# Eleven-product up-projections in two thirds of nine groups, with one room for gates and rotated rows from the fifth unit on

## The chip, the cores and the metric

The kernel runs on one core of a Trainium2 chip. The metric is the device time of one execution in microseconds (us). A core has TensorE (PE: matrix products into PSUM), VectorE (DVE) and ScalarE (ACT) for elementwise work, GpSimd (POOL), SyncE (SP), which here only issues transfers, and 16 DMA engines.

## The reference

A gated linear recurrence feeds a gated feed-forward block, all in 32-bit floats. There are 4 sequences of 768 steps, 8 heads of 48 features; the feed-forward has 3072 tokens, 384 model features and 1536 inner ones.

```
scale = min(mag, 0.999) / (mag + 1e-6)          # mag = |a_re + i a_im|
S = (a * scale) * S + k v^T                     # complex state, per step and head
y = q . Re(S)
x  = y as (3072, 384);  xn = x / rms(x) * rms_g
out = (silu(xn @ w_gate) * (xn @ w_val)) @ w_out
```

## The kernel before

The steps of the recurrence are cut into 24 chunks of 128 tokens (C = 128). Two chunks make a *unit* for the recurrence (the first two units are single chunks, so there are 13) and a *group* for the feed-forward (12 groups of T = 256 tokens).

**A unit.** `load_gates` brings a_re and a_im into the tiles re and im (L674, three transfers each, from SP). `load_rows` brings k, q (L741) and, per chunk, v (L748). `gates` turns re and im by a long chain of ACT and DVE steps on 128x768 elements into cumulated magnitudes and angles: it begins with Square of re (L783), later writes qs at L798, and ends with four products, rot0 to rot3, that rotate k and q into ks, qs, k and q (DVE, L610, the last one `q<-q,y`). `move_rows` copies the rotated rows by 12 transfers a unit into kr and qr (L879), which have features on partitions. Working tiles such as s, w, y, ks and qs have one room each, so the chain of the next unit waits at L798 until the rows of this one have moved. re and im have two rooms, and so have kr and qr: a move waits only for the last y of the unit before the previous one (L888).

**A chunk.** `scores` makes s_ps (PE, L1072), masks it (am, DVE L1077) and transposes kr (kt_ps, L1093). `finish` makes the state (state_ps, L1115, carried on by DVE) and y_ps (L1144). `normalise` makes the root mean square (rs on POOL, L1180) and xT, the scaled input of the feed-forward (DVE, L613); two xT rooms exist, so xT of group g waits for the up-projection of group g-2.

**A group.** The up-projection has 12 inner tiles f of 128 features. A plain tile (L1345) is three contraction blocks for w_gate (wg) and three for w_val (wv), 256 columns each, in one PSUM room "g" of three; then silu (ACT, L1349) and a product (DVE) give hT. In groups 9 to 11 (ELEVEN = 9) `eleven` treats two tiles at once, a *pair* p: for each of the two weights the first two of the three contraction blocks form a 2x2 by 2x2 block product, made with 7 products of 128 columns where 8 would do it plainly, out of sums of weight blocks (S1 to S4, `eleven_sums`) and differences of xT blocks (T, `eleven_inputs`); the third contraction block stays plain with 256 columns. So a weight's pair takes 7 narrow products and two of double width: eleven blocks of 128 columns where the plain way has twelve. The products come in four phases: `one`, `two`, `three`, `four` (L1260). Between phases a partial sum has to leave PSUM: ACT copies it into R (L1284), and DVE adds to R later. Two pairs run in turn, phase by phase, so that one's copy lies under the other's products. Their PSUM rooms are A (from the three "g") and B (from the five "a", which the recurrence uses too).

The output projection (`project`, L1423, from group 2 on) is the same idea with 7 products P1, P2, P6, P7, P5, P3, P4 of six tiles each, sums S1 to S4 of hT on DVE, and copies (ACT, L1445) and adds into ot. P1 starts when the first six tiles of hT are there. Groups 0 and 1 project plainly (L1372).

**What sets the order.** Every step belongs to a lane; `Order.run` plans the kernel ahead of time on estimated durations. Again and again it takes, of all lanes' next steps, the one that could begin first, with a small lateness of its lane (or of the step, `late`) added, and emits it. So each engine's order is fixed when the kernel is built, and at run time engines only wait for one another. `takes` and `gives` count PSUM rooms. `small` reads the weights again at the end (tile `again`, L1040) and takes minima of them on DVE (L1044) for a final check.

Of the kernel before, what the change touches and what calls it, by code (L numbers as in the profile page):

```python
# [568 lines left out]
def fast(tc, ctx, qT, kT, v, a_re, a_im, w_gate, w_val, w_out, rms_g, out, H, bad):  # L569
# [96 lines left out]

    def gate(name, ap, queue, u):
        first_, m = units[u]
        b, c = divmod(first_, NCH)
        if name not in UN[u]:  # L670
            UN[u].update((x, ours(u, x, bufs=2)) for x in ("re", "im"))
        rows = ap[b].rearrange("(h j l) s -> j l h s", j=ND, l=L)
        for j in range(ND):
            queue.dma_start(out=UN[u][name][:, j], in_=rows[j][:, :, c * C:(c + m) * C])  # L674
# [42 lines left out]

    G = [dict() for _ in range(NG)]
# [3 lines left out]
    def load_gates():  # L722
        for u, (first_, m) in enumerate(units):
            for name, ap in (("re", a_re), ("im", a_im)):
                aside = u < 2 and name == "im"
                if (u, name) == (0, "im"):
                    order.ends[name, u] = 8.0
                    continue
                yield step("ACT" if aside else "SP", 0.0 if aside else 3 * order.ISSUE,
                           [("s", units[slots[u - 3][-1]][0])] if u > 2 else [("q", 1)] if u == 2 else [],  # L730
                           lambda name=name, ap=ap, u=u, q=nc.scalar if aside else nc.sync: gate(name, ap, q, u),
                           mb=0.2 * m, ends=[(name, u)])

    def load_rows():
        for u, (first_, m) in enumerate(units):
# [10 lines left out]
            def value(n):  # L746
                U[n]["v"] = vz[n % 4]
                nc.sync.dma_start(out=vz[n % 4][:, :, 0:D],  # L748
# [5 lines left out]
            for n in range(0 if u == 1 else first_, first_ + m) if u else ():  # L754
                yield step("SP", 0.6, [("y", n - 4) if n > 3 else None], lambda n=n: value(n),
# [8 lines left out]
    ELEVEN = 9  # L764
    UPS, OUTS = 0.05, 0.06
# [103 lines left out]
    def move_rows():  # L869
        for u, (first_, m) in enumerate(units):  # L870
            t, two = UN[u], {}

            def move(i, t=t, u=u, two=two, first_=first_, m=m):
                name, rows = ("kr", "qr")[i % 2], (1 - i // 2) * D
                queue = nc.gpsimd if u < ASIDE and i % 2 else nc.sync
                if i < 2:
                    two[name] = sized(unit, name, H, m, p=D2)
# [7 lines left out]
            for i in range(4):  # L885
                aside = u < ASIDE and i % 2
                yield step("POOL" if aside else "SP", 3 * order.ISSUE,
                           [("rot%d" % i, u), ("y", units[u - 1][0] - 1) if u > 1 else None],  # L888
# [131 lines left out]
    def small():  # L1020

        for i, (to, ap, c, f) in enumerate(parts):
# [5 lines left out]
            for half in range(2):  # L1028
# [9 lines left out]
                def get(k=k, n=n, rows=rows, from_=from_):  # L1038
                    raws[k] = prep.tile([P, n], I32, tag="re", name="again", bufs=2)
                    nc.sync.dma_start(out=raws[k].rearrange("p (c f) -> p c f", c=rows), in_=from_)  # L1040
# [6 lines left out]
                yield step("SP", 0.5, [("moved", NU - 1), ("least", k - 2) if k > 1 else ("piece", len(parts) - 1)],  # L1047
# [163 lines left out]
    def eleven_sums():  # L1211

        for i, to in enumerate((wg, wv)):
            a11, a12, a21, a22 = (to[:, :, d, f * P:(f + 1) * P] for f in range(2) for d in range(2))
            for name, tag, x, y, op in (("S1", ("ks", "qs"), a21, a22, ALU.add), ("S2", ("s", "w"), "S1", a11, ALU.subtract),
                                        ("S3", ("y", "r"), a11, a21, ALU.subtract), ("S4", ("p", "k"), a12, "S2", ALU.subtract)):

                def emit(i=i, name=name, tag=tag[i], x=x, y=y, op=op):
                    o = E[name, i] = prep.tile([P, NW * P], FP32, tag=tag, name=name).rearrange("p (f t) -> p f t", f=NW)
                    tt(o, *(E[z, i] if isinstance(z, str) else z for z in (x, y)), op)  # L1220

                yield step("DVE", tt_us(NW * P), [("moved", NU - 1)], emit, ends=[(name, i)])

    def eleven_inputs():

        for g in range(ELEVEN, NG):
# [3 lines left out]
            def inputs(g=g, t=t):  # L1230
                if "T" not in E:
                    E["T"] = prep.tile([P, ND * T], FP32, tag="q", name="T").rearrange("p (a i c) -> p a i c", a=2, i=ND)
                    E["R"] = [prep.tile([P, ND * T], FP32, tag="im", name="R", bufs=2)
                              .rearrange("p (j w c) -> p j w c", j=ND, w=2) for _ in range(2)]
                b11, b12, b21, b22 = t["b"] = [t["xT"][:, d, i * C:(i + 1) * C] for d in range(2) for i in range(2)]
                t1, t2, t4 = t["T"] = [E["T"][:, g % 2, i] for i in range(3)]
                for o, x, y in ((t1, b12, b11), (t2, b22, t1), (b12, b22, b12), (t4, b21, t2)):
                    tt(o, x, y, ALU.subtract)

            yield step("DVE", 4 * tt_us(C), [("xT", last), ("S4", 1), ("up", g - 2)], inputs,  # L1240
                       ends=[("in", g)])

    def eleven(g):
# [5 lines left out]
        def pair(p):  # L1249
# [4 lines left out]
            def product(to, a, b, start=False, stop=False, at=at, p=p):  # L1254

                bank, j = to
                for i, w_ in enumerate((wg, wv)):
                    left = E[a, i][:, p] if isinstance(a, str) else w_[:, p, a[0], a[1] * P:(a[1] + 1) * P]
# [4 lines left out]
            def one(at=at, product=product):  # L1263
                at["A"] = ps_g.tile([P, 2, 2, C], FP32, tag="g", name="up_ps")
                at["r"] = E["R"][p % 2]
# [3 lines left out]
            def two(at=at, product=product):  # L1269
                product(("A", 1), "S2", t["T"][1])  # L1270
                at["B"] = ps_a.tile([P, 2, 2, C], FP32, tag="a", name="up2_ps")
                product(("B", 1), "S3", t["b"][1], start=True)
# [10 lines left out]
            def copied(j, at=at):  # L1283
                nc.scalar.copy(out=at["r"][:, j], in_=at["A"][:, :, 1])  # L1284

            def add(j, bank, block, at=at):
                tt(at["r"][:, j], at[bank][:, :, block], at["r"][:, j], ALU.add)

            def silu(at=at, f1=f1, f2=f2):
                act_ = nc.scalar.activation  # L1290
                act_(out=h[:, f1, C:], in_=at["A"][:, 0, 1], func=AF.Silu)
                act_(out=h[:, f1, 0:C], in_=at["r"][:, 0, 0], func=AF.Silu)

            def silu2(at=at, f2=f2):
                nc.scalar.activation(out=h[:, f2].rearrange("p (i c) -> p i c", i=2), in_=at["r"][:, 1:3, 0], func=AF.Silu)

            def times(at=at, f1=f1):
                tt(h[:, f1, C:], at["A"][:, 1, 1], h[:, f1, C:])
                tt(h[:, f1, 0:C], at["r"][:, 0, 1], h[:, f1, 0:C])

            def times2(at=at, f2=f2):
                o = h[:, f2].rearrange("p (i c) -> p i c", i=2)
                tt(o, at["r"][:, 1:3, 1], o)
# [3 lines left out]
            o, f = (g, f2) if p > 1 else (g - 1, NF + f2)  # L1307
            free = [("h", o, f - 4), ("h", o, f - 5)] if o >= ELEVEN else []
            yield [step("PE", 2 * us, [("in", g)] + ([("out", g - 2)] if p == 0 else []), one, then=0.2, dense=True,
                        ends=[K("1")], takes=("g", 1))]  # L1310
            yield [step("ACT", ac_us(T), [K("1")] + free, lambda c=copied: c(0), ends=[K("p1")])]
            yield [step("PE", 2 * us, [K("p1")], two, then=0.2, dense=True, ends=[K("2")], takes=("a", 1))]
            yield [step("ACT", ac_us(T), [K("2")], lambda c=copied: c(1), ends=[K("u2")])]
            yield [step("PE", 2 * us, [K("u2")], three, then=0.2, dense=True, ends=[K("3")])]
            yield [step("DVE", tt_us(T), [K("u2")], lambda a=add: a(1, "B", 1), ends=[K("u3")])]
            yield [step("ACT", ac_us(T), [K("3")], lambda c=copied: c(2), ends=[K("u4")])]
            yield [step("PE", us + 4 * 2 * pe_us(T), [K("u4"), K("u3")], four, then=0.2, dense=True,
                        ends=[K("4")] + [("up", g)] * (p == NW - 1))]
            yield [step("DVE", tt_us(T), [K("4")], lambda a=add: a(0, "A", 0), ends=[K("c11")]),
                   step("ACT", 2 * ac_us(C), [K("4"), K("c11")], silu, table=["silu"], ends=[K("s1")]),  # L1320
                   step("DVE", 2 * tt_us(T), [K("4")], lambda a=add: (a(1, "B", 0), a(2, "B", 1)), ends=[K("c2")], gives="a"),
                   step("ACT", ac_us(T), [K("c2")], silu2, table=["silu"], ends=[K("s2")]),
                   step("DVE", 2 * tt_us(C), [K("s1")], times, ends=[("h", g, f1)], gives="g"),
                   step("DVE", tt_us(T), [K("s2")], times2, ends=[("h", g, f2)])]

        for p in range(0, NW, 2):

            two = [list(pair(p + i)) for i in range(2)]
            for phase in zip(*two):
                for steps in phase:  # L1330
                    yield from steps

    def feed_forward(groups):
        for g in groups:
            t = G[g]
            for f in range(NF):

                def tile_(f=f, t=t, g=g):
                    t["hT"] = hT[g % 2]
                    t["gv", f] = ps = ps_g.tile([P, 2, T], FP32, tag="g", name="gv_ps")  # L1340
                    busy(flat(ps))
                    cols = slice(f * P % FW, f * P % FW + P)
                    for i, w_ in enumerate((wg, wv)):
                        for d in range(ND):
                            nc.tensor.matmul(ps[:, i], lhsT=w_[:, f * P // FW, d, cols], rhs=t["xT"][:, d],  # L1345
                                             start=d == 0, stop=d == ND - 1)

                def silu(f=f, t=t):
                    nc.scalar.activation(out=t["hT"][:, f], in_=t["gv", f][:, 0], func=AF.Silu)  # L1349

                def times(f=f, t=t):
                    tt(t["hT"][:, f], t["gv", f][:, 1], t["hT"][:, f])

                w_ = [("piece", 2 * (f * P // FW) + i) for i in range(2)]
                free = ([("piece", x) for x in range(2 * NW) if ROOM[x] in ((6, 7), (0, 1))[g]] if g < 2 else [("out", g - 2)]) if f == 0 else []
                yield step("PE", 12 * pe_us(T), w_ + free + [("xT", g * UC + UC - 1)], tile_, then=0.2, dense=True, fills=True,
                           ends=[("gv", g, f)] + [("up", g)] * (f == NF - 1), takes=("g", 1))
                yield step("ACT", ac_us(T), [("gv", g, f)], silu, table=["silu"], ends=[("silu", g, f)])
                yield step("DVE", 0.15 + T / 960, [("silu", g, f)], times, ends=[("h", g, f)], gives="g")
# [207 lines left out]
```

## Time and profile before

| | |
|---|---|
| median of 14 runs | 767.82 us (762.83 to 773.22) |
| the profiled execution, its own time | 765.71 us |
| its span, first to last instruction | 763.6 us, granted TensorE clock 0.984 |
| VectorE busy | 510.0 us (67%) |
| ScalarE busy | 366.2 us (48%) |
| up-projection, plain tiles on TensorE, x1296 | 160.9 + 157.9 us |
| eleven-product pairs, narrow products of T with S, x144 | 22.0 us, mean 275 ns |
| output projection, 128x192 | 85.9 + 42.5 + 21.2 us |
| mean TensorE busy in 200 to 740 us | 538.75 of 540 us |

A line of the groups view reads: source line, engine, operation, output and inputs by their names in the program, shape and count; then busy time and mean duration in ns; then idle time of the engine just before, and which instruction ended most of it. A line of the waits view reads: who waited for whom, in all, how often, the longest. A line of the timeline reads: start, length, engine, line, operation, and how many instructions were merged; an idle time before it stands in brackets. TensorE instructions overlap, so their pace is the distance between starts. Each 32-bit product shows as two instructions.

### The profile page before, as it was taken

The page shows a single profiled execution, that of the slowest core. Times are in us where ns is not written, and L with a number is a line of the kernel's source. Part 1 is how long each engine was busy: PE and PEld are TensorE (multiplying, and loading weights), DVE is VectorE, ACT ScalarE, POOL GpSimd, SP SyncE. Part 2 cuts the span into 40 slices and gives each one's busy share as a digit, 9 for nine tenths or more (in the row PEclk, how much of TensorE's full clock was granted, in tenths as well). Part 3 has the DMA queues.
Part 4 walks back from the last instruction along what each step waited for, and adds up shares of the span by engine and source line. Part 5 has one row for each costly group of instructions (what it writes and reads, how often), then busy time and mean ns, then how long its engine had stood idle before and what let it go on. Part 6 is the DMA issues. An engine that isn't in the chain of part 4 may idle for free. (4 is left out here: it accounts for less than half of the span.)

```text
span 763.6 us, 13411 instructions
## 1 busy us (share of the span) xinstructions
PE 705.3 (92%) x5294; PEld 631.9 (83%) x5294; DVE 510.0 (67%) x997; ACT 366.2 (48%) x640; POOL 50.6 (7%) x93
## 2 busy tenths in 40 slices
PE   0468889999999999999999999999999999999995
PEld 0256568787778999998899899898989999999985
DVE  3979979595576793854869478584586844756462
ACT  5654475566455635464656644547442113233230
POOL 3323000101000000000000000000000000000000
PEclk9987989999999999999999999999999999999998
DMA  7797970945609217365072831907307233233321
GB/s 221 168 186 189 182 194 2 184 128 81 138 1 126 72 23 105 83 74 134 11 126 74 109 80 26 180 14 91 67 16 90 77 100 107 81 114 103 95 94 67
DMA packets 103335, 76.57 MB, mean 100 GB/s; under 512 B 39328, under 2 KB 98464, under 8 KB 103264
## 3 DMA queue, kind: packets, MB, share of 16 engines
q1 hardware_dynamic: 98656, 60.30, 41.2%
q0 software_dynamic: 3744, 14.94, 7.0%
q8 instruction: 43, 0.70, 0.5%
q10 hardware_dynamic: 864, 0.39, 0.2%
q14 instruction: 28, 0.23, 0.1%
HBM read 51.98 MB, written 4.76 MB: 74 GB/s over the span
## 5 line engine op out<-in xcount | busy, mean ns | idle before, releaser
L1345 PE MATMUL gv_ps<-xT,wg 128*128 128x256 f32 x648 | 160.9, 385 | 1.6 <-DVE hT L610 1.6
L1345 PE MATMUL gv_ps<-xT,wv 128*128 128x256 f32 x648 | 157.9, 380 | 2.6 <-DVE wv L610 2.6
L1345 PEld LDWEIGHTS gv_ps<-xT,wv 128*128 128x128 f32 x648 | 123.4, 191 | 19.9 <-DVE wv L610 3.0
L1345 PEld LDWEIGHTS gv_ps<-xT,wg 128*128 128x128 f32 x648 | 120.3, 191 | 20.0 <-issue 2.9
L1349 ACT ACTIVATE hT<-gv_ps 128x256 f32<-128x256 f32 x108 | 40.8, 384 | 149.6 <-PE gv_ps L1345 149.2
L610 DVE TENSOR_TENSOR hT<-gv_ps,hT 128x256 f32<-128x256 f32 x108 | 44.8, 419 | 82.2 <-ACT hT L1349 81.9
L1423 PE MATMUL out_ps<-wo,hT 128*128 128x192 f32 x480 | 85.9, 329 | 3.0 <-ACT ot L1445 3.0
L1423 PEld LDWEIGHTS out_ps<-wo,hT 128*128 128x128 f32 x480 | 78.0, 190 | 5.1 <-ACT ot L1445 4.4
L1072 PE MATMUL s_ps<-qr,kr 96*128 96x128 f32 x384 | 48.3, 279 | 8.4 <-DMA qr<-q 5.2
L1072 PEld LDWEIGHTS s_ps<-qr,kr 96*128 96x128 f32 x384 | 45.6, 192 | 11.3 <-issue 4.0
L610 DVE TENSOR_TENSOR R<-up_ps,R 128x256 f32<-128x256 f32 x72 | 28.7, 421 | 38.4 <-PE up_ps L1260 38.4
L1180 POOL TENSOR_TENSOR rs<-ssq,mhalf 128x1 f32<-128x1 f32 x24 | 20.0, 833 | 514.0 <-DVE ssq L1175 514.0
L1423 PE MATMUL out_ps<-rooms,S 128*128 128x192 f32 x240 | 42.5, 327 | 1.2 <-DVE ot L610 1.2
L1445 ACT COPY ot<-out_ps 128x192 f32<-128x192 f32 x40 | 12.7, 317 | 59.1 <-PE out_ps L1423 58.9
L1423 PEld LDWEIGHTS out_ps<-rooms,S 128*128 128x128 f32 x240 | 39.3, 190 | 2.0 <-DVE ot L610 1.5
L1284 ACT COPY R<-up_ps 128x256 f32<-128x256 f32 x54 | 20.1, 372 | 42.6 <-PE up_ps L1260 41.6
L1260 PE MATMUL up_ps<-xT,wg 128*128 128x128 f32 (+1 forms) x144 | 35.5, 329 | 0.2 <-DVE hT L610 0.2
L1260 PE MATMUL up_ps<-xT,wv 128*128 128x128 f32 (+1 forms) x144 | 35.3, 327 | 0.0
L610 DVE TENSOR_TENSOR ot<-out_ps,ot 128x192 f32<-128x192 f32 x30 | 10.7, 355 | 36.3 <-PE out_ps L1423 19.6
L1077 DVE TENSOR_TENSOR am<-s_ps,causal 128x512 f32<-128x512 f32 x48 | 31.2, 680 | 5.0 <-PE s_ps L1072 4.9
L1349 ACT ACT_TABLE_LOAD x26 | 33.4, 1283 | 0.4
L1372 PE MATMUL out_ps<-wo,hT 128*128 128x384 f32 x96 | 32.6, 490 | 0.0
(170 smaller groups left out, 1207.8 us busy)
## 6 DMA issues: line engine op xcount, KB each, us to landing
k<-in_k_dram SPq DMA_DIRECT2D x24, 192.0 KB, 3.8
q<-in_q_dram SPq DMA_DIRECT2D x24, 192.0 KB, 3.5
vz<-in_v_dram SPq DMA_DIRECT2D x24, 192.0 KB, 3.8
rooms<-in_w_out_dram POOLq DMA_DIRECT2D x6, 768.0 KB, 8.4
out_dram<-ot SPq DMA_DIRECT2D x24, 192.0 KB, 1.9
again<-in_w_gate_dram SPq DMA_DIRECT2D x12, 384.0 KB, 3.6
again<-in_w_val_dram SPq DMA_DIRECT2D x12, 384.0 KB, 3.6
again<-in_w_out_dram SPq DMA_DIRECT2D x12, 384.0 KB, 3.4
```

What stands on the lines that cost most here:

```text
L610: nc.vector.tensor_tensor(out=o, in0=x, in1=y, op=op)
L1072: nc.tensor.matmul(u["s_ps"][a][:, h], lhsT=u["k"][:, a * HH + h], rhs=u["q"][:, a * HH + h], start=True, stop=True)
L1077: nc.vector.tensor_tensor(out=u["am"][a], in0=u["s_ps"][a], op=ALU.mult, in1=causal.unsqueeze(1).to_broadcast([C, HH, C]))
L1180: nc.gpsimd.tensor_tensor(out=u["rs"], in0=u["ssq"], in1=mhalf, op=ALU.pow)
L1260: nc.tensor.matmul(o, lhsT=left, rhs=b, start=start and i == 0, stop=stop, skip_group_check=True)
L1284: nc.scalar.copy(out=at["r"][:, j], in_=at["A"][:, :, 1])
L1345: nc.tensor.matmul(ps[:, i], lhsT=w_[:, f * P // FW, d, cols], rhs=t["xT"][:, d], start=d == 0, stop=d == ND - 1)
L1349: nc.scalar.activation(out=t["hT"][:, f], in_=t["gv", f][:, 0], func=AF.Silu)
L1372: nc.tensor.matmul(t["o_ps", i], lhsT=t["hT"][:, f, i * C:(i + 1) * C], rhs=wo[:, f], start=f == 0, stop=f == NF - 1)
L1423: nc.tensor.matmul(at["ps"][to] if name in ("P7", "P5", "P3", "P4") else at["ps"][:, to], lhsT=left[:, f], rhs=b[:, f], start=start and f ...
L1445: return lambda: nc.scalar.copy(out=out_(i, c), in_=at["ps"][0] if c else at["ps"][:, 0])
```

## The change

Groups 3 to 11 (ELEVEN = 3) use `eleven`, but only for the pairs 0, 1, 3 and 4; the tiles 4, 5, 10 and 11 (pairs 2 and 5) are plain and come after each block of two pairs. The sums S1 to S4 are made once, after the up-projection of group 2; S1 overwrites a weight block in place (those blocks are used by eleven-product groups alone from then on), the others, the copies (R before) and one difference lie in rooms that fall free: one of the two rooms of kr and qr, one of the two of re and im, and the fourth of the v rooms. From unit 5 on (ALONE = 4) re and im, and kr and qr, therefore have one room: gates load only when the unit before is rotated, rows move into kr only after the last scores and transposes of the unit before, into qr only after its last y. v has three rooms from chunk 4 on.

The differences T have one set of rooms and are made after the up-projection of the group before has ended; y of a group from 5 on waits for the up-projection two groups before. P1 of a group from 3 on waits for its whole up-projection. The steps after phase `four` are put in a written-out order, the silu ahead of the add; the steps of a block that are not on PE get a lateness of 0.02, and the lanes' latenesses change (UPS 0.05 to 0.02). The weights are re-read into five rooms instead of two, every other one through POOL, beginning after the last rotation.

```diff
+    ALONE = 4
+    gates_ = {x: [consts.tile([P, ND * T], FP32, name="%s%d" % (x, i)) for i in range(2)] for x in ("re", "im")}
+    turned_ = consts.tile([P, 2, 2, H * T], FP32, name="turned")
+    seconds = turned_[:, 1].rearrange("p a t -> p (a t)")
...
-            UN[u].update((x, ours(u, x, bufs=2)) for x in ("re", "im"))
+            i = (min(u, ALONE) + 1) % 2 if u else 0
...
-                           [("s", units[slots[u - 3][-1]][0])] if u > 2 else [("q", 1)] if u == 2 else [],
+                           [("s", units[slots[u - 3][-1]][0]), ("rot", u - 1) if u > ALONE else None] if u > 2
+                           else [("q", 1)] if u == 2 else [],
...
+    def room_of(n):
+
+        return n % 4 if n < 4 else (n - 4) % 3
...
-    ELEVEN = 9
-    UPS, OUTS = 0.05, 0.06
+    ELEVEN = 3
+    UPS, OUTS = 0.02, 0.06
+    HASTE = 0.02
+    EARLIER = 0
...
-                    two[name] = sized(unit, name, H, m, p=D2)
+                    two[name] = (turned_[0:D2, 0 if u >= ALONE else u % 2, i % 2, 0:H * m * C]
+                                 .rearrange("p (j t) -> p j t", j=H))
...
-                           [("rot%d" % i, u), ("y", units[u - 1][0] - 1) if u > 1 else None],
+                if u > ALONE:
+                    last = first_ - 1
+                    free = [("y", last)] if i % 2 else [("s", last)] + [("kp", last)] * (last % NCH < NCH - 1)
+                else:
+                    free = [("y", units[u - 1][0] - 1)] if u > 1 else []
+                yield step("POOL" if aside else "SP", 3 * order.ISSUE, [("rot%d" % i, u)] + free,
...
-                    raws[k] = prep.tile([P, n], I32, tag="re", name="again", bufs=2)
+                    raws[k] = prep.tile([P, n], I32, tag=("s", "w", "y", "r", "p")[k % 5], name="again")
+                    queue = nc.gpsimd if k % 2 else nc.sync
...
-            yield step("DVE", 4 * tt_us(C), [("xT", last), ("S4", 1), ("up", g - 2)], inputs,
+            yield step("DVE", 4 * tt_us(C), [("xT", last), ("up", g - 1)], inputs,
...
-        for p in range(0, NW, 2):
-
-            two = [list(pair(p + i)) for i in range(2)]
-            for phase in zip(*two):
-                for steps in phase:
-                    yield from steps
+        for p in range(0, NW, 3):
+
+            a, b = (list(pair(p + i)) for i in range(2))
+            for phase in zip(a[:-1], b[:-1]):
+                yield from turns(*phase)
+            plain = [list(tile(g, f)) for f in (2 * p + 4, 2 * p + 5)]
...
+            yield from turns(*((a, b)[i][-1][k:k + 1] for i, k in
+                               [(0, k) for k in (0, 1, 5, 2, 6, 3, 4)] + [(1, k) for k in (1, 0, 5, 2)] + [(0, 7)] +
+                               [(1, k) for k in (6, 3, 4, 7)]))
+            for x in plain:
+                yield from x
...
-        yield pe("P1", a11, b11, 0, True, False, [("h", g, KH - 1)] + [("piece", 2 * NW + i) for i in range(KH // 2)], takes=("g", 1))
+        yield pe("P1", a11, b11, 0, True, False, [("h", g, KH - 1), ("up", g) if g >= ELEVEN else None] + [("piece", 2 * NW + i) for i in range(KH // 2)], takes=("g", 1))
...
-    order.lane(eleven_sums(), 0.0)
-    order.lane(eleven_inputs(), 0.1)
+    order.lane(eleven_sums(), 0.2)
+    order.lane(eleven_inputs(), -1)
```

## The prediction

> **What bounds the kernel now.** I read the page's busy shares first, then TensorE's own waits in the part where it is saturated.
>
> ```profile
> PE 705.3 (92%) x5294; PEld 631.9 (83%) x5294; DVE 510.0 (67%) x997; ACT 366.2 (48%) x640; POOL 50.6 (7%) x93
> ```
> ```profile
> PE out_ps L1423 <- ACT ot L1445: 3.0, 4, 1.5
> PE gv_ps L1345 <- DVE hT L610: 1.6, 1, 1.6
> PE out_ps L1423 <- DVE ot L610: 1.2, 1, 1.2
> PE up_ps L1260 <- DVE hT L610: 0.2, 1, 0.2
> ```
> From 120 us to the end, 6.0 us of waiting in 637: TensorE's work sets the time there, and no wait is for a DMA. What TensorE is relieved of comes off the end, if the work feeding it keeps up. Next its order of time: a plain tile, then a block of two pairs with nothing between them.
>
> ```profile
> 346.08 1.46 PE L1345 MATMUL gv_ps<-xT,wg 128*128 128x256 f32 x6
> 347.37 1.46 PE L1345 MATMUL gv_ps<-xT,wv 128*128 128x256 f32 x6
> 348.67 0.59 PE L1345 MATMUL gv_ps<-xT,wg 128*128 128x256 f32 x2
> ```
> ```profile
> 640.25 0.38 PE L1260 MATMUL up_ps<-xT,wg 128*128 128x128 f32 x2
> 640.47 0.39 PE L1260 MATMUL up_ps<-xT,wv 128*128 128x128 f32 x2
> ...
> 649.52 0.59 PE L1260 MATMUL up_ps<-xT,wv 128*128 128x256 f32 x2
> ```
> Distances between starts count, not durations, which overlap. A plain tile takes 348.67-346.08 = 2.59 us for 12 instructions (a product is two), 0.2158 each; two tiles, 5.18. The block of two pairs runs from 640.25 to 649.52+2x0.2158 = 649.95: 9.70, 4.85 a pair. Check: a pair is 28 instructions of 128 columns at (640.47-640.25)/2, more exactly 0.1117, and 8 of 256: 3.13+1.73 = 4.86.
>
> **The change, part by part.** *Products.* Eleven-product pairs go from 3x6 = 18 to 9x4 = 36. 18 more at 5.18-4.85 = 0.33 us: **-6.0 us** of TensorE work.
>
> [...] Here a column costs 0.1117/(0.2158/2) = 1.035-fold. [...]
>
> *Work given to VectorE and ScalarE.*
>
> ```profile
> L610 DVE TENSOR_TENSOR hT<-gv_ps,hT 128x256 f32<-128x256 f32 x108 | 44.8, 419 | 82.2 <-ACT hT L1349 81.9
> L610 DVE TENSOR_TENSOR R<-up_ps,R 128x256 f32<-128x256 f32 x72 | 28.7, 421 | 38.4 <-PE up_ps L1260 38.4
> L1284 ACT COPY R<-up_ps 128x256 f32<-128x256 f32 x54 | 20.1, 372 | 42.6 <-PE up_ps L1260 41.6
> ```
> A plain pair costs VectorE 2x0.419 = 0.84 us; an eleven-product one 4x0.421, two 128-column products of 0.28 and one of 0.426: 2.67. ScalarE: 2x0.384 = 0.77 against 3x0.372+0.278+0.301+0.417 = 2.11. A middle group has four: VectorE +7.3, with the differences (4x0.288) +8.5; ScalarE +5.4. Over 250 to 600 us the windows show VectorE busy 34 of 50 us, ScalarE 26; in groups of 56 us they become some 83% and 62%. Neither is the bound.
>
> *Waits inside a block.* TensorE now waits on a copy between phases in groups 3 to 8 too: 6 groups x 12 waits. At 640 us the copy ended 0.27 us before its phase began. There ScalarE was nearly free; in the middle it is 62% busy with activations of 0.84 to 0.94 us, some behind a 1.28 us table load. A copy arriving at random finds one with 0 to 0.9 left; beyond the slack that is 0.22 on average, x0.62x72 = 10 us. Behind the waiting product everything on TensorE stands, but the planner sees it and can put another product first: a group has 7 projection steps and some 10 of the recurrence. In groups 9 to 11 this left 0.2 us. Ends 0 and 10; I take **+3**, nearer the measured groups as the filling is the same. It holds the smaller waits too: the differences are now made after the last up-projection of the group before (1.15 us, under two first phases of 1.79; up to 1.4 a group if VectorE sits in a 2.0 us scan), and group 3 waits once for two sums of about 0.7 us, under group 2's projection.
>
> *Tail.* The projection now starts after its whole up-projection. Before, its first product had run early, and at the end:
>
> ```profile
> 742.30 2.22 PE L1423 MATMUL out_ps<-wo,hT 128*128 128x192 f32 x12 [1.50 <-ACT ot L1445]
> 745.68 2.22 PE L1423 MATMUL out_ps<-rooms,S 128*128 128x192 f32 x12 [1.16 <-DVE ot L610]
> ```
> Now two plain tiles end the up-projection, then the first product (1.95) runs over the last silu and multiply (0.38+0.42 and hops, 1.1), the second (1.95) over both sums (2x0.95). Both waits go: **-2.6** (ends 0 and -3).
>
> *Single rooms from the fifth unit on.* These are the danger. The gates' loop:
>
> ```profile
> 474.58 0.84 ACT L783 ACTIVATE s<-re 128x768 f32<-128x768 f32 x1 [1.40 <-DVE qs L610]
> 491.24 0.95 ACT L798 ACTIVATE qs<-re,mid 128x768 f32<-128x768 f32 x1
> 524.46 0.95 DVE L610 TENSOR_TENSOR q<-q,y 128x768 f32<-128x768 f32 x1
> 525.52 0.83 ACT L783 ACTIVATE s<-re 128x768 f32<-128x768 f32 x1
> ```
> Unit follows unit at once: the last rotations lie at 182 and 572 us, eight units, 48.8 each. Now re and im load after the unit before is rotated: six issues of 0.6 and 3.4 to landing, 7 us. But the front part (8.6 to 10 us) today waits for the rows to move before L798: 4.6 to 10.7, mean 7. So the loads cost 0 (hidden there) to 7; ahead of the last row move on SP they delay it by 3.6; I take 4. The stretch from L798 to the rotation, 31 us, holds some 8 us of waiting against 18 us of other VectorE work a group; with 8.5 more, +4. Loop: 48.8+8 = 56.8.
>
> TensorE's period was (649.5-304.1)/6 = 57.6 a group (ends of the up-projections of groups 9 and 3); now 57.6-4x0.33+3/6 = 56.8. The loop just keeps pace, and there is a reserve:
>
> ```profile
> 279.76 0.87 DVE L613 SCALAR_TENSOR_TENSOR xT<-y_ps,gcol,rb 128x128 f32<-128x128 f32 x3 [0.77 <-ACT rb L1188]
> 302.62 1.46 PE L1345 MATMUL gv_ps<-xT,wv 128*128 128x256 f32 x6
> ```
> Group 4's xT is done at 280.6, group 3's up-projection at 304.1: 24 us, perhaps 18 after the first longer loop. Cost **0**; without that cover, each us of the loop beyond 59.3 costs 7 over the seven units left.
>
> [...]
>
> *Other moves.* The row moves wait for the unit before's last products; today those start 9 to 12 us ahead of the rotation (563.4 against 572.4, 272.3 against 284.8). On SP, row loads, decays and output stores stand behind the gates' load; rows are needed some 25 us later: 0. Half the weight re-reads go to POOL, ahead of the last group's rs; its xT was ready 34 us early: 0. Three v rooms for four, an S1 in place: 0.
>
> **Sum.** -6.0+3-2.6 = -5.6. The profiled execution took 765.71 (span 763.6 and 2.1 around it): 760.1. The 14 runs' median is 2.1 above it, 767.82; so **762.2**.
>
> **Rivals.** About 0.3%, 2.3 us, is what a measurement can tell from no change.
>
> *Starved* (0.23): the loop takes 61 us, as the loads' full 7 and 5 of contention give. Then 7x(61-56.8)-18 = +11.4 of TensorE idle before the later groups; with -5.6: +5.8, 773.6. It turns slower past a loop of about 60.5. For it: VectorE at 83%, one long chain, a reserve of only 17 us at group 3 (xT at 230, group 2's up-projection to 247), and two B rooms of the five "a" taken through a block, so that scores, which need two, come later. Against: the loop did one unit in 38 us (386.5 to 424.8), and a starved TensorE leaves VectorE free.
>
> *Stalls within blocks eat it* (0.20): 8 to 10 us of copy waits, unfilled: about -8.6+9, 768. For it the 1.28 us loads, against it groups 9 to 11.
>
> *Everything is filled* (0.10): no stalls, -8.6: 759.2.
>
> Forecast (0.47): 760 to 765 by its own. The change doing nothing is out: the products fall by count. Range 757 to 774: it leaves out the worse half of starvation and an execution at the low end of the 14 (762.83, 5 under their median). Faster 0.56, same 0.16, slower 0.28: the forecast and the filled case, less a little, make faster; starvation and the worst of the stalls make slower.
>
> **What would show it.** Right: 36x28 narrow up_ps products at 0.11; TensorE waits past 120 us under 8 us, a few on R copies; L783 to L783 at 53 to 58 us; no wait between the last products but the 0.4 one. Wrong: waits of gv_ps or up_ps on xT, or of s_ps on qr or kr, in groups 5 to 11 (starved); waits of up_ps on R of over 8 us (stalls); narrow products at 0.13 or more.

## The result, and the profile after

| | before | after |
|---|---|---|
| median of the runs | 767.62 us (47 runs) | 760.15 us (10 runs, 755.50 to 761.23) |
| ratio | | 0.9901, 95% interval 0.9878 to 0.9923 |
| profiled execution: own time, span | 765.71, 763.6 us | 755.36, 753.6 us |
| VectorE, ScalarE busy | 510.0, 366.2 us | 535.1, 382.6 us |

7.5 us faster, between 5.9 and 9.4 by the interval; 5.6 had been forecast. The medians of the experiments below leave out the executions counted as slow (over 1.5% above the fastest of their kernel), two of six of e1 and four of twelve of e10 (783.74 and 775.69 us with them), of which the traces of these two are, so that their losses lie at the upper end. The two profiled executions differ by 10.0 us of span, which is more than the medians do; why is seen below.

First the page of the changed kernel, its busy shares:

```profile
PE 700.7 (93%) x5510; PEld 635.9 (84%) x5510; DVE 535.1 (71%) x1111; ACT 382.6 (51%) x712; POOL 63.4 (8%) x111
```

TensorE runs 216 instructions more, its mix being narrower, and is busy for less; VectorE took 25 us more, ScalarE 16. TensorE's waits from 120 us to the end, in all, how often, the longest:

```profile
PE gv_ps L1403 <- DVE hT L610: 1.7, 1, 1.7
PE out_ps L1487 <- ACT ot L1509: 1.1, 3, 0.5
PE out_ps L1487 <- DVE ot L610: 1.0, 2, 0.5
PE up_ps L1297 <- ACT turned L1322: 0.7, 1, 0.7
PE ss_ps L1214 <- POOL rs L1211: 0.2, 1, 0.2
```

4.7 us for 6.0 before. The copies out of PSUM between phases, which could have stopped TensorE 12 times in each of nine groups, did it once, for 0.7 us. None waits for xT, kr or qr. The timeline of TensorE, two plain tiles of one group and the first and last lines of a pair's first phase in another:

```profile
572.00 1.46 PE L1403 MATMUL gv_ps<-xT,wg 128*128 128x256 f32 x6
...
574.59 1.46 PE L1403 MATMUL gv_ps<-xT,wg 128*128 128x256 f32 x6
```
```profile
452.63 0.39 PE L1297 MATMUL up_ps<-xT,wv 128*128 128x128 f32 x2
...
453.97 0.39 PE L1297 MATMUL up_ps<-xT,wv 128*128 128x128 f32 x2
```

A plain tile is 574.59-572.00 = 2.59 us, as before; 12 narrow instructions lie between the starts 452.63 and 453.97, 0.1117 each, as before. So the work is priced by counts: 432 plain instructions fewer (-93.2 us), 504 narrow ones more (+56.3) and 144 of double width more (+31.1): **-5.8**.

**Where the 10 us of the profiled pair went.** I took all distances between starts on TensorE and subtracted, instruction by instruction, the pace of its kind; what is left is waiting and slow running. Called *loss* below:

| part of the span | before | after | |
|---|---|---|---|
| work, by counts | | | -5.8 |
| loss to 120 us | 31.1 | 27.8 | -3.3 |
| loss 120 to 700 us | 12.3 | 13.5 | +1.2 |
| loss from 700 us | 4.0 | 2.0 | -2.0 |

The first row and the last two make -6.6, which lies within the interval of the medians. The -3.3 ahead of 120 us is not the change's. There TensorE runs the same instructions in the same order in both; before, then after:

```profile
106.25 1.24 PE L1072 MATMUL s_ps<-qr,kr 96*128 96x128 f32 x8 [3.22 <-DVE am L1077]
107.28 2.69 PE L1115 MATMUL state_ps<-vz,kt 128*96 128x48 f32 x16
```
```profile
105.94 1.16 PE L1103 MATMUL s_ps<-turned 96*128 96x128 f32 x8 [1.57 <-DVE am L1108]
106.94 1.48 PE L1146 MATMUL state_ps<-vz,kt 128*96 128x48 f32 x16
```

After a wait of 3.22 us the sixteen state products lasted 2.69 us, after one of 1.57 us 1.48. The clock that TensorE was granted tells them apart. A line here reads: stretch, its length, TensorE's busy time and instructions, granted clock, share of the DMA engines, GB/s. Before, then after:

```profile
88.70:92.10 3.40, 3.40 (x18) 1.00 1.17 140
107.20:114.00 6.80, 6.80 (x81) 0.50 0.28 55
```
```profile
88.70:92.10 3.40, 3.40 (x10) 0.51 1.13 144
107.20:114.00 6.80, 6.80 (x112) 1.00 0.27 52
```

In the kernel before, the clock was halved for 6.8 us behind the long wait. In the profiled execution of the changed kernel it was halved for 3.4 us at 88.7 already: TensorE lost some 1.7 us there (half of that, an estimate), came to the wait that much later, waited 1.65 us less and kept its full clock behind it. The experiments (all with the same start of the kernel) show both cases: e5 has the early halving and a wait of 1.59 us, the other eleven have the long wait and the late halving. So this part of the start falls differently from one execution to the next, and only what comes after 120 us is compared below. From there to the last product the granted clock is 1.00 in both kernels, so the rest of the difference is not the clock's. The changed kernel's runs form two clusters (four at 755.5 to 758.5, six at 760.1 to 761.2) about as far apart; its one trace, at 755.36, has the short wait, and there is none of the upper cluster.

The tail, where two waits of 1.50 and 1.16 us stood:

```profile
733.11 2.22 PE L1487 MATMUL out_ps<-wo,hT 128*128 128x192 f32 x12 [0.45 <-ACT ot L1509]
735.83 2.22 PE L1487 MATMUL out_ps<-rooms,S 128*128 128x192 f32 x12 [0.51 <-DVE ot L610]
```

And the gates' loop: end of one unit's rotation, Square of the next re, Abs (qs), next rotation, next Square.

```profile
409.98 0.95 DVE L610 TENSOR_TENSOR q<-q,y 128x768 f32<-128x768 f32 x1
418.21 0.85 ACT L808 ACTIVATE s<-re 128x768 f32<-128x768 f32 x1
431.51 0.92 ACT L823 ACTIVATE qs<-re,mid 128x768 f32<-128x768 f32 x1
465.66 0.95 DVE L610 TENSOR_TENSOR q<-q,y 128x768 f32<-128x768 f32 x1
474.00 0.85 ACT L808 ACTIVATE s<-re 128x768 f32<-128x768 f32 x1 [1.96 <-DMA re<-in_a_re_dram]
```

Before, the Square began within 2 us of the last rotation's start; now it begins 8.2 us after it and waits for a transfer. The loop is 56.6 us a unit (from 178.2 to 631.2 us, eight units), and yet no wait of TensorE comes of it.

### The profile page after: what moved, and what is told of

The parts are those of the page before. It is cut to its first block, busy times and chain, and to the rows that moved or that the text cites. A ratio compares the mean times of both kernels' runs of the same rounds, so it can differ in the third digit from the quotient of the medians.

```text
span 753.6 us, 14032 instructions
## 1 busy us (share of the span) xinstructions
PE 700.7 (93%) x5510; PEld 635.9 (84%) x5510; DVE 535.1 (71%) x1111; ACT 382.6 (51%) x712; POOL 63.4 (8%) x111
## 4 chain that ended last, share of the span: by engine, by line
PE 85%; DVE 4%; DMA 4%; ACT 2%; issue 1%; POOL 1%; DVEq 0%; ACTq 0%; POOLq 0%
PE up_ps L1297 23%; PE gv_ps L1403 23%; PE out_ps L1487 18%; PE y_ps L1175 6%; PE s_ps L1103 5%; PE out_ps L1436 4%; PE state_ps L1146 3%; DMA rooms<-in_w_out_dram 2%; PE kt_ps L1124 2%; DMA turned<-q 1%; PE ss_ps L1214 1%; PE ss_ps L1202 0%; DVE p L835 0%; DVE wg L613 0%; DVE wg L610 0%
## 5 line engine op out<-in xcount | busy, mean ns | idle before, releaser
L1403 PE MATMUL gv_ps<-xT,wg 128*128 128x256 f32 x432 | 108.2, 387 | 1.7 <-DVE hT L610 1.7
L1403 PE MATMUL gv_ps<-xT,wv 128*128 128x256 f32 x432 | 105.6, 380 | 2.6 <-DVE wv L610 2.6
L1403 PEld LDWEIGHTS gv_ps<-xT,wv 128*128 128x128 f32 x432 | 82.4, 191 | 14.3 <-DVE wv L610 3.0
L1403 PEld LDWEIGHTS gv_ps<-xT,wg 128*128 128x128 f32 x432 | 80.8, 193 | 15.4 <-DVE hT L610 2.1
L1297 PE MATMUL up_ps<-xT,wg 128*128 128x256 f32 (+1 forms) x288 | 71.2, 329 | 0.0
L1297 PE MATMUL up_ps<-xT,wv 128*128 128x256 f32 (+1 forms) x288 | 70.7, 327 | 0.0
L610 DVE TENSOR_TENSOR hT<-gv_ps,hT 128x256 f32<-128x256 f32 x72 | 30.0, 418 | 37.6 <-ACT hT L1407 37.5
L1103 PE MATMUL s_ps<-turned 96*128 96x128 f32 x384 | 49.4, 283 | 6.9 <-DMA turned<-q 5.4
L1103 PEld LDWEIGHTS s_ps<-turned 96*128 96x128 f32 x384 | 46.9, 196 | 9.2 <-issue 3.7
L1297 PEld LDWEIGHTS up_ps<-xT,wv 128*128 128x128 f32 x288 | 49.2, 191 | 3.7
L1297 PEld LDWEIGHTS up_ps<-xT,wg 128*128 128x128 f32 x288 | 47.0, 191 | 2.6 <-issue 0.8
L1322 ACT COPY turned<-up_ps 128x256 f32<-128x256 f32 x72 | 26.6, 370 | 33.4 <-PE up_ps L1297 32.6
L610 DVE TENSOR_TENSOR ot<-out_ps,ot 128x192 f32<-128x192 f32 x30 | 10.6, 354 | 32.0 <-issue 15.5
L1108 DVE TENSOR_TENSOR am<-s_ps,causal 128x512 f32<-128x512 f32 x48 | 31.1, 680 | 2.6 <-PE s_ps L1103 2.6
```

The source lines that it names most:

```text
L610: nc.vector.tensor_tensor(out=o, in0=x, in1=y, op=op)
L1103: nc.tensor.matmul(u["s_ps"][a][:, h], lhsT=u["k"][:, a * HH + h], rhs=u["q"][:, a * HH + h], start=True, stop=True)
L1108: nc.vector.tensor_tensor(out=u["am"][a], in0=u["s_ps"][a], op=ALU.mult, in1=causal.unsqueeze(1).to_broadcast([C, HH, C]))
L1297: nc.tensor.matmul(o, lhsT=left, rhs=b, start=start and i == 0, stop=stop, skip_group_check=True)
L1322: nc.scalar.copy(out=at["r"][j], in_=at["A"][:, :, 1])
```

## The experiments

The theory at the start: TensorE's products set the time, and the single rooms cost nothing as long as the loop of the gates keeps pace with TensorE. The rival: the gain comes from the new order of the work (latenesses, waits, the tail), the products being beside the point. Each was timed beside the kernel before. "Loss" is TensorE's from 120 us on, in one profiled execution each; "waits" is its idle time there, and "clock" is half of the time in which its granted clock was 0.50, an estimate of what that cost (1.6 to 2.1 us of it in e1, e10, e11 and e12 is the end of the halving that began at 107). What is left of the loss, some 8 to 20 us, is not traced.

| kernel | median, us | ratio to before, 95% | loss after 120 us | waits | clock |
|---|---|---|---|---|---|
| before | 767.62 | | 16.3 | 6.0 | 0 |
| after | 760.15 | 0.9878 to 0.9923 | 15.5 | 4.7 | 0 |
| e1_groups9to11 | 782.10 | 1.0122 to 1.0229 | 30.7 | 13.8 | 8.7 |
| e2_groups6to11 | 796.30 | 1.0318 to 1.0415 | 48.9 | 26.1 | 8.5 |
| e3_project_first | 814.53 | 1.0575 to 1.0649 | 67.5 | 37.5 | 10.2 |
| e4_early_p1_last | 760.18 | 0.9879 to 0.9943 | 16.5 | 5.6 | 0 |
| e5_plain3to8 | 773.03 | 1.0043 to 1.0107 | 23.8 | 10.7 | 1.7 |
| e6_chain4 | 775.85 | 1.0058 to 1.0128 | 32.6 | 15.9 | 1.7 |
| e7_outs0 | 780.34 | 1.0128 to 1.0194 | 37.1 | 18.6 | 5.1 |
| e8_gaterooms | 765.24 | 0.9949 to 0.9996 | 13.1 | 3.5 | 0 |
| e9_early_load | 768.29 | 0.9986 to 1.0052 | 24.8 | 11.1 | 1.7 |
| e10_chain4_early | 775.17 | 1.0057 to 1.0133 | 33.7 | 15.8 | 5.5 |
| e11_earlier1 | 798.68 | 1.0355 to 1.0445 | 58.1 | 30.4 | 10.1 |
| e12_nine_early | 770.40 | 1.0002 to 1.0066 | 17.8 | 6.3 | 1.8 |

**One thing holds for all but e4.** The order is planned anew for each kernel, so an edit comes with another order on every engine. Set beside the changed kernel's, 12 of TensorE's 5,510 instructions stand elsewhere in e4 and none of VectorE's or ScalarE's; in e9, whose edit is one word, some 1,250 of TensorE's do, 290 of VectorE's 1,111 and 180 of ScalarE's 712. Such a run prices an edit together with its new order.

**Fewer groups with eleven products** (e1, e2). The count of products is the dose: 12 pairs in e1 and 24 in e2, where the changed kernel has 36 and the kernel before 18.

```diff
-    ELEVEN = 3
+    ELEVEN = 9        # e2: 6
```


> The changed kernel with eleven-product pairs from group 9 on only (ELEVEN = 9): 12 pairs where the changed kernel has 36 and the kernel before 18; the single rooms, the new tail and the five rooms for the re-reads stay. Theory of work (the gain is TensorE's products at 0.33 us a pair, rooms cost nothing): 24 pairs fewer, +8.0 us on 760.15, so 768.1. Rival, everything else made the gain (tail, order, re-reads): it stays at 759 to 763. Rival, the single rooms cost something that the products pay for: above 770.

> The same with ELEVEN = 6: 24 pairs, 12 fewer than the changed kernel. Theory of work: +4.0, 764.1, half way between the changed kernel and the run with 12 pairs. If stalls within the blocks of the middle groups ate part of each pair's gain, the step from 24 to 36 pairs would be smaller than the one from 12 to 24.

Both missed widely: 782.1 and 796.3. The dose was swamped: e1's loss after 120 us is 15 us above the changed kernel's, e2's 33. TensorE's waits in e1:

```profile
PE out_ps L1487 <- ACT ot L1509: 5.3, 3, 4.5
...
PE ss_ps L1202 <- ACT w L882: 2.1, 1, 2.1
...
PE gv_ps L1403 <- DVE xT L613: 1.6, 2, 0.8
```

There xT is late, and so is w (L882), a step of the gates' chain: waits of the kind that the prediction's rival named, but with *fewer* eleven-product groups. It is not that rival's slow loop, though: e1's loop is 56.6 us on average, as in the changed kernel, and from group 3 on xT is ready 10 us or more before the up-projection of the group before ends. In the longest wait, the 4.5 us up to 378.6, the copy that TensorE waits for stands on ScalarE behind steps of the gates' chain:

```profile
373.21 0.84 ACT L813 ACTIVATE y<-re 128x768 f32<-128x768 f32 x1
...
375.70 0.93 ACT L820 ACTIVATE p<-r,ones 128x768 f32<-128x768 f32 x1
...
378.22 0.31 ACT L1509 COPY ot<-out_ps 128x192 f32<-128x192 f32 x1
```

**Plain tiles in groups 3 to 8, the rest as in the changed kernel** (e5; its first lines stand in `eleven`, the others in the sums and the differences).

```diff
         for p in range(0, NW, 3):
+        if g < 9:
+            for f in range(NF):
+                yield from tile(g, f)
+            return
...
-                yield step("DVE", ..., there + ([("up", ELEVEN - 1)] if name == "S1" else []), emit,
+                yield step("DVE", ..., there + ([("up", 8)] if name == "S1" else []), emit,
...
-        for g in range(ELEVEN, NG):
+        for g in range(9, NG):
```


> The changed kernel with its lanes and waits as they are, but in groups 3 to 8 all tiles plain; the sums are made after group 8's up-projection. 12 pairs, as in the run with ELEVEN = 9, which came to 783.74 with TensorE waiting in 360 to 420 us. Theory of work: 24 pairs fewer than the changed kernel, +8.0, 768.1; then the rest of that run's loss came from its order (two plain lanes and a projection that need not wait). Rival, the single rooms starve plain groups in any order: 775 to 785 with waits on xT or rs.

773.0, between the two. 24 pairs fewer are 24x0.33 = 7.9 us of products; measured +12.9 over the changed kernel, of which 8.3 is loss after 120 us. So the products' count and some 5 to 8 us of waiting and halved clock, which came with the other order, are both in it.

**Two rooms for re and im again, in e1** (e8). The load may then run a unit ahead, as before the change; kr and qr keep their one room.

```diff
-            i = (min(u, ALONE) + 1) % 2 if u else 0
+            i = (u + 1) % 2 if u else 0
-                           [("s", ...), ("rot", u - 1) if u > ALONE else None] if u > 2
+                           [("s", ...)] if u > 2
```


> The run with ELEVEN = 9 (783.74), but the gates keep two rooms to the end and load ahead as before; kr and qr stay single from unit 5 on. If the gates' load behind the rotation made that run starve: back to about 768, Square of re at once after each rotation. If the single kr and qr did: it stays at 778 to 785.

765.2: 16.9 us came back, and the loss is the lowest of all, 13.1. One room for kr and qr has no visible price; that for re and im, with the order that came with it, was what slowed e1. This kernel has six pairs *fewer* than the one before (+2.0 us of products) and is still 2.4 faster (0.3 to 3.9 by its interval): the rest of the change, its order and its tail, is worth some 4 us by itself, 3.2 by the losses.

**A longer chain** (e6): four more ScalarE copies of 0.84 us, each onto itself, in the middle of every unit's chain from unit 5 on.

```diff
             yield E("ACT", ac_us(n1), [K("sums")], ..., K("whole"))
+            for _ in range(4 if u > ALONE else 0):
+                yield E("ACT", ac_us(n1), [], lambda: act_(out=w, in_=w, func=AF.Copy), K("whole"))
```


> The changed kernel with four more copies of 128x768 on ScalarE (0.84 us each, w onto itself) in the gates' chain of units 5 to 12: the loop is 3.4 us a unit longer. Theory that the loop just keeps pace (55.4 us a unit against TensorE's 55.4, xT ready 8.9 us early): 8x3.4 = 27 less 9 of reserve, up to +18, 770 to 778, with TensorE waiting in the recurrence. Rival, the loop follows TensorE and its waits absorb this: 759 to 763.

775.85, 15.7 us over the changed kernel, for 3.4 us in each of eight units off TensorE. The loop became 60.4 us, and xT of groups 7 to 10 came between 7.2 us after and 1.2 us before the end of the up-projection of the group before. This fits the theory that the loop just keeps pace. A rival, that the copies themselves hold ScalarE, is put to the test in e10.

**The load let go earlier** (e9; e10 is e6 with it, e12 is e1 with it). The last readers of re and im are the sines; the load need not wait for the rotation.

```diff
-                           [("s", ...), ("rot", u - 1) if u > ALONE else None] if u > 2
+                           [("s", ...), ("sin", u - 1) if u > ALONE else None] if u > 2
```


> The changed kernel, in which re and im load once the sines and cosines of the unit before are made (they are the last readers) instead of once its rows are rotated, some 4 to 8 us earlier. Theory (the loop of the gates only just keeps pace and costs no time of its own): the loop from rotation to rotation falls from 56.6 to some 52 us a unit where it is free to, xT comes earlier, and the time stays within 2 us of the changed kernel's 760.2. Rival (the loads' 8 us a unit are on the path that sets the end): 3 us or more off, under 757.

> The kernel with four more ScalarE copies in every unit's chain from the fifth unit on (775.9 us), and the loads of re and im let go at the sines instead of at the rotation. Theory (what that kernel lost, it lost to a loop of 60.4 us a unit that is longer than TensorE's period of some 56.6): the earlier loads give back 3 to 8 us a unit, the loop is at or under 57.5, and the time falls to 761 to 768. Rival (the copies themselves hold ScalarE, in front of the copies out of PSUM and the silus): 773 to 777, as before.

> The kernel with eleven products in groups 9 to 11 alone and everything else of the change (783.7 us), and the loads of re and im let go at the sines instead of at the rotation. Keeping two rooms for them brought it to 765.2. Theory (the load standing behind the rotation starves it): half or more of that comes back, 764 to 774. Rival (the place of the load doesn't matter, two rooms helped because the load could run a whole unit ahead): 779 to 786.

e12 met its theory (770.4; 11.7 of the 16.9 us that two rooms gave back). e9 met neither theory nor rival: 768.3, which is 8 us *worse* than the changed kernel. e10 came out where its rival had it, 775.2, nothing back, although its loop fell from 60.4 to 57.9 us and xT was ready 15 us or more ahead from group 4 on. So it is not shown that e6 lost its 15.7 us to its loop; the copies' place on ScalarE, or the new order, would do as well. Where did the loop's 8 us go in e9 and e12? Means over the eight units, from start to start, us:

| | rotation to Square | Square to Abs | Abs to rotation | loop |
|---|---|---|---|---|
| before, L783 and L798 | 0.3 | 15.9 | 32.6 | 48.8 |
| after, L808 and L823 | 8.4 | 14.2 | 34.0 | 56.6 |
| e8, two rooms | 0.3 | 15.9 | 32.6 | 48.8 |
| e9, early load | 1.4 | 19.1 | 35.0 | 55.5 |
| e12, early load | 1.3 | 19.6 | 35.3 | 56.1 |

The wait for the load went, 7 us of it, and nearly as much came back at other places of the chain. One such place in e12, on ScalarE:

```profile
411.95 0.38 ACT L1407 ACTIVATE hT<-gv_ps 128x256 f32<-128x256 f32 x1
...
415.00 0.38 ACT L1407 ACTIVATE hT<-gv_ps 128x256 f32<-128x256 f32 x1 [2.27 <-PE gv_ps L1403]
419.54 0.38 ACT L1407 ACTIVATE hT<-gv_ps 128x256 f32<-128x256 f32 x1 [4.16 <-PE gv_ps L1403]
422.13 0.38 ACT L1407 ACTIVATE hT<-gv_ps 128x256 f32<-128x256 f32 x1 [2.21 <-PE gv_ps L1403]
422.42 0.93 ACT L823 ACTIVATE qs<-re,mid 128x768 f32<-128x768 f32 x1
```

Abs (L823) waits for the rows to have moved; the last of them landed at 413.3. But in ScalarE's written order Abs stands behind the silus, and the last three of these wait for TensorE's tiles, one after the other. Here the chain is tied to TensorE's pace by its place in the queue, not by data. So the theory that the loop *sets* what TensorE gets holds in one direction only: in the single-room kernels the loop also follows TensorE (55.0 us a group in the changed kernel, from 302.2 to 687.1 us, where the loop's last six units take 55.1 each; 55.9 a group in e9), and a load's 8 us cannot be read off as 8 us of loop. e9's 8 us are 6.4 us more of waits and 1.7 of halved clock. Why the early load brings them in e9, and not in e12, stays open: the waits are small and of other kinds (ss_ps on rs 4.3 us in four, gv_ps on hT 3.7 in four), and its order is another one throughout.

**The order by itself** (e3, e7, e11). e3 and e7 set the projection's lateness; e11 lets the first plain tile of a block go ahead of the block's closing steps.

```diff
-    UPS, OUTS = 0.02, 0.06
+    UPS, OUTS = 0.02, -3.0      # e7: 0.0
...
-    EARLIER = 0
+    EARLIER = 1                 # e11 alone
```


> Lateness of the output projection's lane -3.0 instead of 0.06: the planner takes a projection product as soon as it can, and keeps none to fill the waits between the phases of a block. Theory that filling hides the copy waits: 3 to 10 us longer, 763 to 770, with waits of up_ps on copies in the profile. Rival, the copies come in time anyway since the slack of 0.27 us suffices: within 2 us of 760.15.

> Lateness of the projection's lane 0.0 instead of 0.06 (UPS stays 0.02): of two products that could begin at once the projection's goes first, but TensorE is not kept waiting for it, as -3.0 did. Theory that kept projection products fill the waits: 3 to 10 us longer than 760.15. Rival, only the deliberate waiting of the -3.0 run cost its 54 us: 759 to 763.

> The changed kernel, with the first of the two plain tiles of each block let go ahead of the closing steps of the two pairs, in the order written out. Theory (TensorE hardly waits inside blocks, about 1 us in all): within 2 us of 760.2. Rival (the closing steps are what holds PSUM rooms and so the next products): 2 us or more off.

814.5, 780.3 and 798.7, with not one product more or fewer. I had expected the projection's products to fill waits on the copies inside the blocks. e7 says otherwise:

```profile
PE ss_ps L1202 <- DVE sq L610: 7.6, 4, 3.1
...
PE up_ps L1297 <- ACT turned L1322: 1.7, 2, 1.1
```

With the filling gone only 1.7 us of waits on copies appear, and 7.6 on sq, a step of `normalise` behind the recurrence: it is there that the kept-back products seem to be missed most. In e3 TensorE also stands waiting for the projection's own copies and sums (12.7 us of out_ps on ot, beside 12.0 of ss_ps on rs), so that its 54 us are no price of the filling alone. In e11 one wait shows how a loss becomes longer than the wait:

```profile
608.34 0.49 PE L1124 MATMUL kt_ps<-ident,turned 96*128 96x96 f32 x4
612.14 0.90 PE L1124 MATMUL kt_ps<-ident,turned 96*128 96x96 f32 x4 [3.30 <-ACT kt L1128]
...
613.74 1.06 PE L1297 MATMUL up_ps<-xT,wg 128*128 128x256 f32 x2
614.59 1.06 PE L1297 MATMUL up_ps<-xT,wv 128*128 128x256 f32 x2
```

After 3.30 us of waiting two instructions of 256 columns take 614.59-613.74 = 0.85 us where 0.43 is their pace. The granted clock is 0.50 from 611.3 to 618.1:

```profile
611.30:618.10 6.80, 5.96 (x23) 0.50 0.05 2
```

**The tail** (e4): the last group's first projection product no longer waits for its up-projection.

```diff
-   ("up", g) if g >= ELEVEN else None
+   ("up", g) if ELEVEN <= g < NG - 1 else None
```


> The last group's first projection product is again free to run before its up-projection has ended; all other groups as in the changed kernel. Theory of the tail (the first product, kept for the end, covers the last silu, multiply and sum): +1 to +2.5 us, 761 to 762.7, and waits of over 1 us between the last projection products come back. Rival (the gain at the tail comes from the plain tiles at the end, whose silu and multiply are short): within 0.7 us of 760.15, with no such wait.

```profile
737.53 2.22 PE L1487 MATMUL out_ps<-wo,hT 128*128 128x192 f32 x12 [0.68 <-ACT ot L1509]
740.90 2.22 PE L1487 MATMUL out_ps<-rooms,S 128*128 128x192 f32 x12 [1.15 <-DVE ot L610]
```

The median is the same (760.18), as the rival had it. The trace shows that the waits do grow, from 0.45 and 0.51 to 0.68 and 1.15; the loss from 700 us on is 2.85 for 1.97, 0.9 us, which the medians don't resolve. So of the tail's 2.0 us this wait is worth about half, and the rest is not traced to a single edit.

None of the twelve beats the changed kernel. Of the theory and the rival at the start, both have a share: from e8 to the changed kernel 24 pairs are added, 7.9 us by the count, and with 2.4 us more loss 5.5 are to be expected and 5.1 are measured; from the kernel before to e8 the products go the wrong way and 2.4 us are gained.

## Why the prediction was right, point by point

- **Products, -6.0: right, -5.8.** The pace of a narrow product did not change with 1,008 of them: 0.1117 us, mean record 275 to 278 ns. The price taken from the trace's rows held.
- **Waits inside blocks, +3 (ends 0 and 10): mis-sized, +1.2** for the whole of 120 to 700 us. The term charged a random arrival on a 62% busy ScalarE; its copies were placed by the planner, and one of 108 waits showed. ScalarE was busy 29.2 of 50 us in 250 to 600 us (58%), VectorE 36.4 (73%, for 83% forecast). The 83% added the pairs' work to a stretch of the profile in which the loop still ran a unit in 48.8 us; at 56.6 the gates' own work per microsecond falls. Steps that overlap in the records made the rest: VectorE's busy time grew by 25 us and the sum of its durations by 36, where the prediction's own count (18 pairs at 2.67-0.84 = 1.83 and six sets of differences at 1.15) makes 40.
- **Tail, -2.6: right, -2.0.** The two waits of 1.50 and 1.16 fell to 0.45 and 0.51; I had them at nothing.
- **The single rooms, 0: right in time, wrong in the margin.** The loop was forecast at 56.8 and is 56.6, by two errors that cancel, so that the match is luck: the front part, rotation to Abs, grew by 6.4 us (4 forecast), the stretch from Abs to the rotation by 1.4 (4 forecast). The loads of re took 5.9 us to land, not 3.4, issued as they were between the row moves (2.6 in e9, ahead of them). The reserve was the weakest step. I had put it at 24 us, perhaps 18 after the first longer loop; it is 11.8 us there, and 8.0 or 8.1 for each of the groups 5 to 10. For group 9 xT is ready at 569.1:

```profile
568.26 0.86 DVE L613 SCALAR_TENSOR_TENSOR xT<-y_ps,gcol,rb 128x128 f32<-128x128 f32 x3
```

and group 8's up-projection ends at 577.2. A lead that is the same six times over is not a stock being used up, as I had it; it fits two chains that keep step in a written order. The price of going past it, "each us of the loop beyond 59.3 costs 7", makes 7.7 us for e6's loop of 60.4, where 15.7 were measured; how much of these the loop took is open after e10.
- **The rival *Starved*** (773.6) did not come about here. Waits of its kind do occur in e1, but without its loop of 61 us: a late step in the written order was enough there. e8 against e1 makes the second room of re and im worth 16.9 us together with its order, while no wait of TensorE in the changed kernel is for its absence. That the single rooms cost nothing is thus true of this order and was not foreseen as such.
- **The forecast of 762.2 against 760.15**: of the 2.0 us, 1.8 is the term for the blocks; the products' 0.2 and the tail's 0.6 are small and go the other way. The remaining 1 us is within what the runs resolve.

What the prediction did not see is that the gain depends on one particular order. The same products in other orders (e3, e7, e9, e11) measure 768 to 814 us.

## What to carry to other kernels

Price removed work at the pace that the trace shows for the very same shape, by counts; that term held within 0.2 us. When a second buffer is given up, don't ask only whether the loop still keeps pace, but how far ahead its result is at each use, and what stands behind the loop's steps in the written order: here 8 us of lead was enough, while e9 and e10, with 15 us and more from group 4 on, were slower. And where a planner writes the order, an edit of one word moves more than a thousand instructions: a variant's time is the price of edit and order together, so keep the order fixed (as e4 nearly does) or don't read a part's price from it.

## What the runs showed of the hardware that was not expected

- A wait of TensorE can be followed by products at half pace (0.85 us for 0.43 in e11), and then the granted clock is 0.50. Behind the wait of 3.22 us at 106.25 us in the kernel before it was so for 6.8 us, which at half pace loses 3.4 us, an estimate, more than the wait itself. In e12, behind a wait of 3.22 us at 106.63, six instructions of 256 columns still took 121.70-119.00 = 2.70 us, where 1.30 is their pace:

```profile
119.00 2.91 PE L1403 MATMUL gv_ps<-xT,wg 128*128 128x256 f32 x6
121.70 2.44 PE L1403 MATMUL gv_ps<-xT,wv 128*128 128x256 f32 x6
```

- The length of the wait alone did not tell what came behind it. Ahead of the same product at 87 us TensorE waited 2.61 us in the kernel before and 2.60 in the changed one; before, then after:

```profile
87.67 1.56 PE L1345 MATMUL gv_ps<-xT,wv 128*128 128x256 f32 x6 [2.61 <-DVE wv L610]
```
```profile
87.41 1.67 PE L1403 MATMUL gv_ps<-xT,wv 128*128 128x256 f32 x6 [2.60 <-DVE wv L610]
```

  From 88.7 to 92.1 us the granted clock was 1.00 in the first and 0.51 in the second. In e2 TensorE was idle for 3.40-1.46 = 1.94 us in 545.6 to 549.0, and the clock was 0.50 in the next 10.2 us:

```profile
545.60:549.00 3.40, 1.46 (x12) 1.00 0.00 0
549.00:559.20 10.20, 10.20 (x46) 0.50 0.01 2
```

  What decides it, and how long it lasts, is open.
- The same load of 128 KB lands in 5.9 us (median of re; 5.3 for im) when it is issued between the row moves, in the changed kernel from 180 to 640 us, and in 2.6 us (2.9 for im) when ahead of them, in e9.
